# One matmul kernel, first token block computed with unsplit 32-bit operands, the weights' two parts made later

## The chip, the cores and the metric

The kernel runs on one core of one Trainium2 chip. The metric is the device time of one execution in microseconds (us), as the median of several executions. The engines are PE (matrix multiply), ACT (ScalarE), DVE (VectorE), POOL (GpSimd) and SP, which here only issues transfers.

## The reference

Three layers run one after the other on 4608 tokens of width 512:

```
q_s = softmax(q, axis=-1);  k_s = softmax(k, axis=tokens)      # 8 batches, 8 heads, 576 x 64
x   = q_s @ (k_s.T @ v)                                        # linear attention, heads joined to 512
h   = x @ w_in;  x = (h * cos(h)) @ w_out                      # 512 -> 2048 -> 512
do  = x @ w_skip > 0;  e = argmax(x[do] @ w_gate)              # 8 experts
out = x;  out[do] += gate * (relu(x @ w1[e]) @ w2[e])          # 512 -> 1024 -> 512
```

`w_in` and `w_out` come as 64-bit floats, all else as 32-bit floats.

## The kernel before

Tokens are taken in 12 blocks of 384. For each block the attention gives `xT`, the transposed input, and then 16 units follow, one for each 128 columns of the 2048. Unit `n` of the program is unit `c = n % 16` of block `j = n // 16`. In unit `n` PE runs `h_mm(n)` (12 matmuls of 384 columns, the h-tile), then `out_mm(n-3)` (9 matmuls of 512 columns into three accumulators `o`); `LAG = 3` is that distance. Between them lie `chain_a` and `chain_b` (h times cos h, on ACT and DVE) and `chain_c` (the product in two parts). The second expert stage (another matmul pair with its own loops) follows after the 12 blocks.

A product of 32-bit numbers is made from three matmuls in the faster type `float32r`: each operand is held as a high part (a cast on ACT) and a low part (a subtraction on DVE or POOL), and high-high, high-low and low-high are added. So x (`xh`, `xl`), the chain's product (`gh`, `gl`), the attention's kv matrix (`kvbh`, `kvbl`), q (`qh`, `ql`) and the weights (`W[m]`) all exist in two parts.

The 32 weight tiles `m` (even: a `w_in` slice for unit m/2, odd: a `w_out` slice) are loaded once, as 64-bit numbers, by `w_load`. `w_turn(m, done)` makes a 32-bit number from the bits (L148 on ACT, L149 and L154 on DVE, L155 on POOL) and, two steps later, splits the finished tile (L143 on ACT, L152 on DVE or, for tiles listed in `LOP`, on POOL). `w_step` does one such step; the tables `WA`, `WB`, `WC` say how many steps stand at which place of a unit of block 0, and `FP` where the next block's attention stands. The tile order is `order`: 0, 2, 4, then 1, 6, 3, 8 and so on. All engines run their instructions in the order in which the code writes them; there is no scheduler. The attention of block `j+1` is spread over the units of block `j` (`attention`, with the unit numbers in `A1` for block 1). In block 0 it also holds PE's, ACT's and DVE's time beside the weights.

Ahead of the first unit stands the attention of block 0 itself: `kmax_a` to `kmax_c`, `k_exp`, `kv_mm` for k and v, `q_max`, `q_exp`, `q_norm`, `q_trans`, `x_make` for q. `warm` issues matmuls on zeros.

Of the kernel before, what the change touches and what calls it, by code (L numbers as in the profile page):

```python
# [21 lines left out]
P = 128  # L22
# [20 lines left out]
A1 = (3, 3, 4, 6, 7, 9, 9, 9, 10, 8)  # L43
# [29 lines left out]
def body(ctx, tc, q, k, v, w_in, w_out, wg, w1, w2, cf, ct, ci, out):  # L73
# [51 lines left out]
    cw = {}  # L125
# [11 lines left out]
    def w_turn(m, done):  # L137


        if done is not None:  # L140
            f = cw.pop(done).bitcast(F32)
            t = W[done] = wp.tile([P, 2, DM], F32R, tag=f"w{done}", name="w")
            nc.scalar.copy(t[:, 0, :], f)  # L143
        if m is not None:
            w = cw[m].bitcast(U32).rearrange("p (n t) -> p n t", t=2)
            lw, hw = w[:, :, 0], w[:, :, 1]
            u = cw[m] = ws.tile([P, DM], U32, tag="u", name="u", bufs=4)
            nc.scalar.activation(lw, lw, AF.Copy, scale=2.0 ** -29)  # L148
            nc.vector.tensor_scalar(u, hw, 3, 0x3FFFFFF8, op0=ALU.logical_shift_left, op1=ALU.bitwise_and)  # L149
        if done is not None:  # L150
            eng = nc.gpsimd if done in LOP else nc.vector
            eng.tensor_tensor(t[:, 1, :], f, t.bitcast(F32)[:, 0, :], op=ALU.subtract)  # L152
        if m is not None:
            nc.vector.scalar_tensor_tensor(hw, hw, 0xC0000000, u, op0=ALU.bitwise_and, op1=ALU.bitwise_or)  # L154
            nc.gpsimd.tensor_tensor(u, hw, lw, op=ALU.add)  # L155
# [5 lines left out]
    at = [0]  # L161

    def w_step(n=1):
        for _ in range(n):
            t = at[0]
            at[0] += 1
            w_turn(order[t] if t < len(order) else None, order[t - 2] if 2 <= t < len(order) + 2 else None)
            if t + AHEAD < len(order):
                w_load(order[t + AHEAD])
# [54 lines left out]
    def kv_mm(b, i0=0, i1=NP):  # L224
        t, vv, n = kt, vt.rearrange("p c (h e) -> p c h e", h=H), i1 - i0
        ps = misc()[:, 0:n * (D + 1)].rearrange("p (i e) -> p i e", i=n)
        for i in range(n):
            for c in range(5):
                for u in range(2):
                    h = 2 * (i0 + i) + u  # L230
                    nc.tensor.matmul(ps[u * D:(u + 1) * D, i, :], t[:, c, h * D:(h + 1) * D], vv[:, c, h, :],
                                     start=c == 0, stop=c == 4)
        z = sp.tile([P, NP], F32, tag="kz", name="kz")[:, 0:n]
        nc.vector.tensor_scalar(z, ps[:, :, D], 1e-9, None, op0=ALU.add)
        nc.vector.reciprocal(z, z)
        t = sp.tile([P, DM], F32, tag="km", name="kv")[:, 0:n * D].rearrange("p (i e) -> p i e", i=n)
# [29 lines left out]
    def x_new(j):  # L266
        xT[j] = {s: p2.tile([P, KD, TB], F32R, tag="x" + s, name="x" + s) for s in "hl"}
# [24 lines left out]
    def q_trans(j, i):  # L292
        if j > 1:
            t = qt[j].rearrange("p g h d -> p (g h d)")[:, i * TB:(i + 1) * TB]
        else:
            t = (misc() if j else ps_h.tile([P, TB], F32, tag="h", name="h"))[:, 0:TB]
            for g in range(NG):
                nc.tensor.transpose(t[:, g * P:(g + 1) * P], qt[j][:, g, 2 * i:2 * i + 2, :].rearrange("p h d -> p (h d)"), ident)
        qT = st["qT", j, i] = {s: sp.tile([P, TB], F32R, tag="q" + s, name="q" + s, bufs=2) for s in "hl"}
        split(t, qT["h"], qT["l"])  # L300

    def x_make(j, i):
        qT = st.pop(("qT", j, i))
        ps = misc()
        c0 = 0
# [12 lines left out]
    def h_mm(n):  # L318
        j, c = divmod(n, NC)
        Hp[n] = ps_h.tile([P, TB], F32, tag="h", name="h")  # L320
        seq = [(a, b, kk) for kk in range(KD) for a, b in (("h", "h"), ("h", "l"), ("l", "h"))]
        for t, (a, b, kk) in enumerate(seq):
            nc.tensor.matmul(Hp[n], win(a, kk, c), xT[j][b][:, kk, :],  # L323
                             start=t == 0, stop=t == len(seq) - 1)
# [6 lines left out]
    def chain_b(n):  # L331
# [12 lines left out]
    def out_mm(n):  # L344
# [4 lines left out]
        for g in range(NG):  # L349
            for t, (a, b) in enumerate((("h", "h"), ("h", "l"), ("l", "h"))):  # L350
# [36 lines left out]
    def logits(j, rp):  # L387
# [5 lines left out]
        lt = R["lt", j] = rp.tile([P, TB], F32, tag="lt", name="lt", bufs=1)  # L393
# [112 lines left out]
    def init_table():  # L506
        z = ws.tile([P, E * CAP // P // 2, 2], I32, tag="z", name="z", bufs=1)
# [108 lines left out]
    def mlp(mp):  # L616
        XG = [mp.tile([P, G2, DM], F32, name=f"xg{i}") for i in range(2)]
# [254 lines left out]
    with tc.manual_schedule():  # L872
# [3 lines left out]
        for t in (kt, vt):  # L876
            nc.gpsimd.memset(t[64:P, 4, :], 0.0)
        for t in kvb:
            for s in "hl":
                nc.vector.memset(t[s].bitcast(F32), 0.0)  # L880
        load_k(0, 0, 2)
        load_q(0)
        load_k(0, 2, 4)
        load_v(0, 0, 2)
        for m in order[0:6]:
            w_load(m)
        load_v(0, 2, 4)
        for m in order[6:AHEAD]:
            w_load(m)
        nc.sync.dma_start(cfs, cf)  # L890
        nc.sync.dma_start(cis, ci)
        nc.sync.dma_start(tri, ct)
        nc.sync.dma_start(wgs, wg.rearrange("(k p) e -> p k e", p=P))
# [27 lines left out]
        x_make(0, 1)
        q_trans(0, 3)
        w_step()
        x_make(0, 2)
        x_make(0, 3)
        N = NB * NC
        for n in range(N + LAG):
# [32 lines left out]
            if j == 0:  # L960
                w_step(WB[c])
# [15 lines left out]
            if j == 0:  # L977
                w_step(WC[c])
# [94 lines left out]
```

## Time and profile before

| | |
|---|---|
| median of 3 executions | 1254.25 us (1253.8 to 1258.02) |
| the profiled execution | 1256.17 us, of which the span (first to last instruction) is 1254.3 us |
| PE, DVE, ACT, POOL busy | 96%, 60%, 57%, 33% of the span |
| TensorE's granted clock, mean | 0.986 of full speed |

The shares are means over the whole span. PE's 96% comes from a long stretch in which it never stops; the change lies in the first tenth of the span, where it does stop. The time of an execution is 1.9 us more than its span.

### The profile page before, as it was taken

Reading aid. Unit: us, or ns where it says so; the run is one execution under the profiler, and the core shown is the slowest. Engines: PE = TensorE matmul, PEld = TensorE weight load, DVE = VectorE, ACT = ScalarE, POOL = GpSimd, SP = SyncE. Lnnn points to the kernel's source line nnn. Section 1 sums busy time; section 2 is a strip of 40 time slices with the busy share of each in tenths; the row PEclk is TensorE's granted clock in tenths of the full one; section 3 lists DMA queues with packets and bytes.
Section 4 is the critical chain, followed back from the end, with each engine's and each line's share of the span. In section 5 each row is a group of like instructions: output and inputs, shape, how many; then the busy total and the mean of one; then the engine's idle time right before and its main releaser. Section 6 shows DMA issues by size and latency. Waiting matters only on the chain. (4 is left out here: it accounts for less than half of the span.)

```text
span 1254.3 us, 19798 instructions
## 1 busy us (share of the span) xinstructions
PE 1200.4 (96%) x7028; PEld 1056.8 (84%) x7028; DVE 752.6 (60%) x1506; ACT 719.3 (57%) x1393; POOL 411.5 (33%) x365
## 2 busy tenths in 40 slices
PE   7777999999999999999999999999999999999986
PEld 4666898888899898989988888898888889999984
DVE  7999735556354545635455564535565976676661
ACT  3667655655666665566655566665575555555541
POOL 3666542334324233432423334232120222122121
PEclk8889999999999999999999999999999999999998
DMA  9920222224212222321323232221054676677653
GB/s 306 366 82 1 58 39 69 51 65 110 48 56 51 73 57 64 109 34 61 59 36 97 65 97 35 73 51 26 26 168 144 184 244 226 220 227 235 214 153 146
DMA packets 209493, 138.75 MB, mean 111 GB/s; under 512 B 138200, under 2 KB 173272, under 8 KB 209376
## 3 DMA queue, kind: packets, MB, share of 16 engines
q1 hardware_dynamic: 204272, 125.13, 36.1%
q0 software_dynamic: 5104, 12.17, 2.8%
q8 instruction: 60, 0.98, 0.3%
q14 instruction: 57, 0.47, 0.1%
HBM read 106.35 MB, written 15.95 MB: 97 GB/s over the span
## 5 line engine op out<-in xcount | busy, mean ns | idle before, releaser
L323 PE MATMUL h<-xh,w 128*128 128x384 f32 x1536 | 435.9, 345 | 20.6 <-DVE w L152 6.6
L351 PE MATMUL o<-w,gh 128*128 128x512 f32 x1152 | 363.2, 396 | 2.6 <-ACT x L363 2.6
L323 PEld LDWEIGHTS h<-xh,w 128*128 128x128 f32 x1536 | 284.2, 190 | 38.3 <-DVE w L152 9.6
L342 POOL TENSOR_TENSOR gl<-a,gh 128x384 fp32r<-128x384 f32 x176 | 184.8, 1050 | 394.5 <-ACT gh L340 289.2
L323 PE MATMUL h<-xl,w 128*128 128x384 f32 x768 | 261.7, 341 | 0.1
L351 PEld LDWEIGHTS o<-w,gh 128*128 128x128 f32 x1152 | 214.8, 189 | 39.2 <-ACT x L363 3.9
L351 PE MATMUL o<-w,gl 128*128 128x512 f32 x576 | 229.0, 397 | 1.8 <-POOL gl L342 1.8
L335 DVE SCALAR_TENSOR_TENSOR a<-a,h 128x384 f32<-128x384 f32 x192 | 104.7, 545 | 191.9 <-ACT a L334 191.8
L328 ACT ACTIVATE a<-h 128x384 f32<-128x384 f32 x192 | 93.1, 485 | 182.5 <-PE h L323 106.2
L329 DVE SCALAR_TENSOR_TENSOR a<-a,h 128x384 f32<-128x384 f32 x192 | 105.4, 549 | 140.0 <-ACT a L328 139.9
L323 PEld LDWEIGHTS h<-xl,w 128*128 128x128 f32 x768 | 146.2, 190 | 5.6 <-DVE xl L314 0.6
L340 ACT CAST gh<-a 128x384 fp32r<-128x384 f32 x192 | 97.9, 510 | 72.4 <-DVE a L335 72.4
L844 PE MATMUL h<-xh,w 128*128 128x256 f32 x704 | 137.4, 280 | 0.3 <-DVE w L123 0.3
L351 PEld LDWEIGHTS o<-w,gl 128*128 128x128 f32 x576 | 108.5, 188 | 29.9 <-POOL gl L342 3.4
L123 DVE TENSOR_TENSOR w<-wr,w 128x512 fp32r<-128x512 f32 x192 | 123.9, 688 | 7.4 <-ACT w L122 1.9
L844 PEld LDWEIGHTS h<-xh,w 128*128 128x128 f32 x704 | 113.3, 189 | 4.1 <-ACT w L122 0.7
L855 PE MATMUL o<-w,gh 128*128 128x512 f32 x352 | 112.9, 401 | 0.0
L122 ACT CAST w<-wr 128x512 fp32r<-128x512 f32 x192 | 108.7, 618 | 1.8 <-DMA wr<-in_w 1.7
L333 ACT ACTIVATE a<-a 128x384 f32<-128x384 f32 x192 | 100.7, 524 | 11.0 <-DVE a L329 10.7
L334 ACT ACTIVATE a<-a 128x384 f32<-128x384 f32 x192 | 100.9, 525 | 6.1
L847 ACT ACTIVATE gh<-h 128x256 fp32r<-128x256 f32 x88 | 33.8, 384 | 120.4 <-PE h L844 96.9
L844 PE MATMUL h<-xl,w 128*128 128x256 f32 x352 | 98.7, 280 | 0.0
(220 smaller groups left out, 1460.1 us busy)
## 6 DMA issues: line engine op xcount, KB each, us to landing
wr<-in_w SPq DMA_DIRECT2D x101, 512.0 KB, 4.3
qt<-in_q SPq DMA_DIRECT2D x12, 768.0 KB, 5.7
out<-x SPq DMA_DIRECT2D x36, 256.0 KB, 2.2
wr<-in_w_in SPq DMA_DIRECT2D x16, 512.0 KB, 9.8
wr<-in_w_out SPq DMA_DIRECT2D x16, 512.0 KB, 11.2
xl<-x SPq DMA_DIRECT2D x160, 48.0 KB, 2.1
xh<-qt SPq DMA_DIRECT2D x160, 48.0 KB, 2.1
vt<-in_v SPq DMA_DIRECT2D x7, 1040.0 KB, 5.8
```

The costliest lines, as they stand in the source:

```text
L122: nc.scalar.copy(hi, src)
L123: nc.vector.tensor_tensor(lo, src, hi.bitcast(F32), op=ALU.subtract)
L323: nc.tensor.matmul(Hp[n], win(a, kk, c), xT[j][b][:, kk, :], start=t == 0, stop=t == len(seq) - 1)
L329: nc.vector.scalar_tensor_tensor(a, a, MAGIC, Hp[n], op0=ALU.subtract, op1=ALU.subtract)
L333: nc.scalar.activation(a, a, AF.Sin, scale=PI)
L334: nc.scalar.activation(a, a, AF.Square)
L335: nc.vector.scalar_tensor_tensor(a, a, 0.5, Hp.pop(n), op0=ALU.subtract, op1=ALU.mult)
L340: nc.scalar.copy(G[n]["h"], a)
L342: eng.tensor_tensor(G[n]["l"], a, G[n]["h"].bitcast(F32), op=ALU.subtract)
L351: nc.tensor.matmul(O[j][g], gg[a][:, g * P:(g + 1) * P], wout(b, c), start=c == 0 and t == 0, stop=c == NC - 1 and t == 2)
L844: nc.tensor.matmul(ps, win2(a, kk, c0, c * P, P), xt[b][:, kk, 0:T2], start=t == 0, stop=t == len(seq) - 1)
L855: nc.tensor.matmul(o[g], g_[a][:, g * P:(g + 1) * P], wout(b, c0 + c), start=c == 0 and t == 0, stop=c == NF - 1 and t == 2)
```

## The change

Block 0 does without the two parts. `x_new(0)`, `x_make(0, i)`, `q_trans(0, i)`, `h_mm`, `chain_b` and `out_mm` keep single 32-bit tiles (`xf`, `qf`, `kvf`, `gf`, and the turned weight `F[m]`) when `j == 0`, and one 32-bit matmul stands where three `float32r` matmuls stood. `w_turn` only turns; `F[m]` is written in place over the loaded tile. The split is a function of its own, `w_split`, called by `w_parts`: one tile in each unit from unit 4 to unit 15, then two and one in turn in block 1, always on ACT and DVE; a spare buffer (`SPARE`) lets a split tile go where the tile before it lay. `kv_parts` makes the two parts of kv for block 1 in unit 1.

Each unit of block 0 now has two `w_step`s at fixed places. Ahead of the units the order changes: both halves of k are loaded before q, the subtraction of q's maximum and half of `q_norm` run on DVE for block 0, ACT's table loads are called for early by a one-column instruction (`dum`), v's second half is loaded ahead of all but one weight, and `h_mm(0)` is issued in two halves. `init_table` (POOL) and four small loads move into unit 1, and its tile `z` now shares a buffer with `km`, the tile in which `kmax_a` takes its maxima. `lt` and one input tile of the last stage share other buffers.

```diff
+    def w_turn(m):
+        a = cw.pop(m)
...
+        u = ws.tile([P, DM], U32, tag="u", name="u", bufs=2)
+        nc.scalar.activation(lw, lw, AF.Copy, scale=2.0 ** -29)
+        nc.vector.tensor_scalar(u, hw, 3, 0x3FFFFFF8, op0=ALU.logical_shift_left, op1=ALU.bitwise_and)
+        nc.vector.scalar_tensor_tensor(hw, hw, 0xC0000000, u, op0=ALU.bitwise_and, op1=ALU.bitwise_or)
+        nc.gpsimd.tensor_tensor(a.bitcast(U32)[:, 0:DM], hw, lw, op=ALU.add)
+        F[m] = a.bitcast(F32)[:, 0:DM]
+
+    def w_split(m):
+        f = F.pop(m)
+        t = W[m] = wp.tile([P, 2, DM], F32R, tag="w" + room_w.pop(0), name="w")
+        nc.scalar.copy(t[:, 0, :], f)
+        nc.vector.tensor_tensor(t[:, 1, :], f, t.bitcast(F32)[:, 0, :], op=ALU.subtract)
+        room_w.append(str(m))
...
+    def kv_parts():
+        for u in range(2):
+            r = slice(u * D, (u + 1) * D)
+            hi, lo = (kvb[0][s][r, :, r] for s in "hl")
+            split(kvf[r, :, r], hi, lo)
...
     def x_make(j, i):
+        if j == 0:
+            nc.tensor.matmul(ps[:, 0:TB], kvf[:, i, :], qT["f"], start=True, stop=True)
+            nc.scalar.activation(xT[j]["f"][:, i, :], ps[:, 0:TB], AF.Copy, scale=INV2PI)
+            return
...
+        for kk in range(k0, k1):
+            if j == 0:
+                nc.tensor.matmul(Hp[n], F[2 * c][:, kk * P:(kk + 1) * P], xT[j]["f"][:, kk, :],
+                                 start=kk == 0, stop=kk == KD - 1)
+                continue
...
+        g = a
+        if n < NC:
+            g = p3.tile([P, TB], F32, tag="gh", name="gf")
+            G[n] = {"f": g}
+        nc.vector.scalar_tensor_tensor(g, a, 0.5, Hp.pop(n), op0=ALU.subtract, op1=ALU.mult)
...
+            if j == 0:
+                nc.tensor.matmul(O[j][g], gg["f"][:, g * P:(g + 1) * P], F[2 * c + 1], start=c == 0, stop=c == NC - 1)
+                continue
...
+        z = sp.tile([P, DM], F32, tag="km", name="z").bitcast(I32)[:, 0:2 * n].rearrange("p (c t) -> p c t", t=2)
...
+        q_max(0, 0)
+        kmax_b(0, 2, 4)
+        q_max(0, 1)
+        q_exp(0)
+        warm(4)
+        kmax_c(0, 2, 4)
+        k_exp(0, 2, 4)
+        nc.scalar.activation(dum, dum, AF.Sin)
+        warm(4)
+        kv_mm(0, 0, 2)
+        q_norm(0)
+        warm(4)
+        kv_mm(0, 2, 4)
+        w_step()
+        warm(4)
+        q_trans(0, 0)
+        x_new(0)
+        q_trans(0, 1)
...
+        x_make(0, 2)
+        h_mm(0, 0, 2)
         w_step()
-        x_make(0, 2)
         x_make(0, 3)
+        h_mm(0, 2, 4)
...
-                w_step(WB[c])
+                w_step()
...
-                w_step(WC[c])
+            if n >= SPL and at[1] < 2 * NC:
+                w_parts(1 if n < NC or c % 2 else 2)
+            if n == 1:
+                init_table()
+                kv_parts()
```

What the change does to the instructions shows in the order on three engines. On PE, where the attention ends and the first units begin, the program before has the last group of x (three matmuls of the two parts of kv and q), then the h-tile of unit 0 from parts of x and of the weight:

```order
L310 MATMUL m<-qh,kvbh_91 128x384
L310 MATMUL m<-ql,kvbh_91 128x384
L310 MATMUL m<-qh,kvbl_92 128x384
L323 MATMUL h<-xh,w 128x384
L323 MATMUL h<-xl,w 128x384
L323 MATMUL h<-xh,w 128x384 x2
```

In the changed program the same place reads as follows; `wr` is the loaded tile, in which the turned weight now lies:

```order
L320 MATMUL h<-ident,qt 128x128 x3
L332 MATMUL m<-qf,kvf 128x384
L357 MATMUL h<-xf,wr 128x384 x2
L332 MATMUL m<-qf,kvf 128x384
L357 MATMUL h<-xf,wr 128x384 x14
L395 MATMUL o_452<-wr,gf 128x512
```

One matmul stands for three, the first half of unit 0's h-tile moved ahead of the last group of x, and nothing but turned weights is waited for there.

On DVE, unit 4 of block 0 before (the chain's two instructions, then turns L149 and L154 around a split L152):

```order
L335 SCALAR_TENSOR_TENSOR a<-a,h 128x384
L329 SCALAR_TENSOR_TENSOR a<-a,h 128x384
L149 TENSOR_SCALAR u<-wr 128x512
L154 SCALAR_TENSOR_TENSOR wr<-wr,u 128x512
L149 TENSOR_SCALAR u<-wr 128x512
L152 TENSOR_TENSOR w<-u,w 128x512
L154 SCALAR_TENSOR_TENSOR wr<-wr,u 128x512
```

and the same unit in the changed program (L202 is one step of the next block's `kmax_a`):

```order
L377 SCALAR_TENSOR_TENSOR gf<-a,h 128x384
L367 SCALAR_TENSOR_TENSOR a<-a,h 128x384
L142 TENSOR_SCALAR u<-wr 128x512
L143 SCALAR_TENSOR_TENSOR wr<-wr,u 128x512
L142 TENSOR_SCALAR u<-wr 128x512
L143 SCALAR_TENSOR_TENSOR wr<-wr,u 128x512
L202 TENSOR_TENSOR km<-km,kt 128x512
L152 TENSOR_TENSOR w<-wr,w 128x512
```

The split moved to the unit's end, where the tile that it makes is first read in block 1.

On POOL, in units 3 to 6 of block 0 before, the turn's addition (L155), the product's low part (L342) and the splits listed in `LOP` (L152) take turns:

```order
L155 TENSOR_TENSOR u<-wr 128x512 x2
L342 TENSOR_TENSOR gl<-a,gh 128x384
L152 TENSOR_TENSOR w<-u,w 128x512
L155 TENSOR_TENSOR u<-wr 128x512 x2
L342 TENSOR_TENSOR gl<-a,gh 128x384
L152 TENSOR_TENSOR w<-u,w 128x512
```

and in the changed program, from the last turn ahead of unit 2 on (L557, L558 and L561 are `init_table`, L265 is block 1's `q_max`):

```order
L144 TENSOR_TENSOR wr<-wr 128x512 x7
L557 MEMSET z 128x152
L558 MEMSET z 128x152
L561 DMA tab<-z 128x304 x2
L144 TENSOR_TENSOR wr<-wr 128x512 x10
L265 TENSOR_TENSOR qt<-qt,qm 128x1536
L144 TENSOR_TENSOR wr<-wr 128x512 x6
```

Low parts and splits left POOL for the whole of block 0, and the table's transfer moved from ahead of the units to behind the seventh turn.

## Rows read from the trace of the kernel before

**Rows 1.** Busy time of each engine by stage, with granted clock and DMA.
```profile
core 0: us, PE busy (x) PEld busy (x) DVE busy (x) ACT busy (x) POOL busy (x), PEclk, DMA share, GB/s
0.00:32.42 32.42, 23.54 (x150) 14.07 (x151) 24.58 (x46) 13.02 (x23) 11.12 (x17) 0.84 0.97 308
32.42:45.92 13.50, 8.96 (x37) 7.49 (x37) 12.17 (x18) 7.14 (x15) 6.70 (x6) 0.87 1.05 353
45.92:138.85 92.93, 72.37 (x402) 61.37 (x402) 89.67 (x117) 62.63 (x120) 66.03 (x51) 0.93 0.31 105
138.85:206.00 67.15, 67.15 (x345) 59.91 (x344) 31.52 (x70) 40.75 (x78) 24.38 (x22) 1.00 0.20 36
```

**Rows 2.** PE's timeline: start and length in us; units 0, 3, 16, 17 begin.
```profile
32.42 0.34 PE L323 MATMUL h<-xh,w 128*128 128x384 f32 x1
...
45.92 0.44 PE L323 MATMUL h<-xh,w 128*128 128x384 f32 x1 [2.51 <-DVE a L335]
...
138.85 0.34 PE L323 MATMUL h<-xh,w 128*128 128x384 f32 x1
...
140.97 0.63 PE L351 MATMUL o<-w,gh 128*128 128x512 f32 x2
...
143.06 0.34 PE L323 MATMUL h<-xh,w 128*128 128x384 f32 x1
```

**Rows 3.** PE's waits from 32.4 to 139 us: total, times, longest.
```profile
PE h L323 <- DVE w L152: 6.6, 7, 2.2
PE h L323 <- DVE a L335: 5.9, 3, 2.5
PE h L323 <- POOL w L152: 5.1, 2, 4.1
```

**Rows 4.** 32-bit matmuls: ns min/median/max of a record, then runs of PE's timeline.
```profile
L392 PE MATMUL m<-x,wgs x80: 486/498/510, 189.3 to 858.0; 128*32 128x384 f32 x80
...
L214 PEld LDWEIGHTS m<-ident,kmx x64: 187/190/337, 7.6 to 754.0; 128*128 128x128 f32 x64
L214 PE MATMUL m<-ident,kmx x64: 271/275/582, 7.6 to 754.1; 128*128 128x128 f32 x64
...
88.83 1.05 PE L214 MATMUL m<-ident,kmx 128*128 128x128 f32 x8
...
101.98 2.55 PE L231 MATMUL m<-vt,kt 128*64 128x65 f32 x80
```

**Rows 5.** Groups by line, 32.4 to 140 us: busy us, mean ns, idle before.
```profile
L154 DVE SCALAR_TENSOR_TENSOR wr<-wr,u 128x512 uint32<-128x512 uint32 x30 | 34.7, 1157 | 0.3
L152 DVE TENSOR_TENSOR w<-u,w 128x512 fp32r<-128x512 f32 x20 | 23.5, 1174 | 1.1 <-ACT w L143 0.9
L149 DVE TENSOR_SCALAR u<-wr 128x512 uint32<-128x512 uint32 x29 | 15.7, 542 | 0.0
...
L155 POOL TENSOR_TENSOR u<-wr 128x512 uint32<-128x512 uint32 x30 | 36.2, 1206 | 29.1 <-issue 7.8 <-DVE wr L154 5.2 <-ACT xh L313 4.7
L152 POOL TENSOR_TENSOR w<-u,w 128x512 fp32r<-128x512 f32 x10 | 16.7, 1675 | 2.1 <-DVE a L329 1.6 <-ACT w L143 0.5
L342 POOL TENSOR_TENSOR gl<-a,gh 128x384 fp32r<-128x384 f32 x14 | 16.4, 1169 | 2.4 <-ACT gh L340 2.4
```

**Rows 6.** DVE and POOL timelines near 49 us.
```profile
48.82 0.41 DVE L149 TENSOR_SCALAR u<-wr 128x512 uint32<-128x512 uint32 x1
49.15 0.68 DVE L152 TENSOR_TENSOR w<-u,w 128x512 fp32r<-128x512 f32 x1
49.75 1.53 DVE L154 SCALAR_TENSOR_TENSOR wr<-wr,u 128x512 uint32<-128x512 uint32 x1
...
49.12 1.60 POOL L155 TENSOR_TENSOR u<-wr 128x512 uint32<-128x512 uint32 x1 [1.38 <-ACT a L333]
```

**Rows 7.** DVE and ACT timelines ahead of the first unit.
```profile
10.66 2.73 DVE L200 TENSOR_TENSOR km<-kt 128x256 f32<-128x256 f32 x1 [0.46 <-DMA kt<-in_k]
...
17.03 1.74 DVE L255 TENSOR_REDUCE qs<-qt 128x24 f32<-128x1536 f32 x1
...
26.87 0.49 ACT L313 ACTIVATE xh<-m 128x384 fp32r<-128x384 f32 x1
27.38 1.28 ACT L918 ACT_TABLE_LOAD   x1
```

**Rows 8.** DMA issues up to 150 us: KB each, median us to landing.
```profile
tab<-z POOLq DMA_DIRECT2D x2, 152.0 KB, 5.6
```

**Rows 9.** PE's waits from 139 to 275 us.
```profile
PE o L351 <- POOL gl L342: 0.8, 1, 0.8
PE o L351 <- ACT x L363: 0.6, 1, 0.6
```

More of the change, by code (lines that the diff above doesn't have):

```diff
@@ L123, in split @@
         nc.vector.tensor_tensor(lo, src, hi.bitcast(F32), op=ALU.subtract)
-    cw = {}
+    cw, F = {}, {}
+    room_w = [f"x{i}" for i in range(SPARE)]
     def w_load(m):
@@ L135, in w_load @@
             nc.sync.dma_start(a, w_out[c * P:(c + 1) * P, :])
[L137 to L155, printed above, removed]
+    def w_turn(m):
+        a = cw.pop(m)
+        w = a.bitcast(U32).rearrange("p (n t) -> p n t", t=2)
+        lw, hw = w[:, :, 0], w[:, :, 1]
+        u = ws.tile([P, DM], U32, tag="u", name="u", bufs=2)
[10 more added lines that the diff above has]
+        room_w.append(str(m))
     order = [0, 2, 4]
@@ L160, in body, with w_parts @@
     order = [m for m in order if m < 2 * NC]
-    at = [0]
+    at = [0, 0]
     def w_step(n=1):
[L164 to L169, printed above, removed]
+        for m in order[at[0]:at[0] + n]:
+            w_turn(m)
+        for m in order[at[0] + AHEAD:at[0] + n + AHEAD]:
+            w_load(m)
+        at[0] += n
+    def w_parts(n=1):
+        for m in order[at[1]:at[1] + n]:
+            w_split(m)
+        at[1] += n
     qt = {}
@@ L316, in body, with h_mm @@
     A, G, Hp, O = {}, {}, {}, {}
-    def h_mm(n):
+    three = (("h", "h"), ("h", "l"), ("l", "h"))
+    def h_mm(n, k0=0, k1=KD):
         j, c = divmod(n, NC)
[L320 to L324, printed above, removed]
+        if k0 == 0:
+            Hp[n] = ps_h.tile([P, TB], F32, tag="h", name="h")
+        for kk in range(k0, k1):
+            if j == 0:
+                nc.tensor.matmul(Hp[n], F[2 * c][:, kk * P:(kk + 1) * P], xT[j]["f"][:, kk, :],
+                                 start=kk == 0, stop=kk == KD - 1)
+                continue
+            for t, (a, b) in enumerate(three):
+                nc.tensor.matmul(Hp[n], win(a, kk, c), xT[j][b][:, kk, :],
+                                 start=kk == 0 and t == 0, stop=kk == KD - 1 and t == 2)
     def chain_a(n):
@@ L349, in out_mm @@
         for g in range(NG):
[L350 removed]
+            if j == 0:
+                nc.tensor.matmul(O[j][g], gg["f"][:, g * P:(g + 1) * P], F[2 * c + 1], start=c == 0, stop=c == NC - 1)
+                continue
+            for t, (a, b) in enumerate(three):
                 nc.tensor.matmul(O[j][g], gg[a][:, g * P:(g + 1) * P], wout(b, c),
@@ L616, in mlp @@
     def mlp(mp):
-        XG = [mp.tile([P, G2, DM], F32, name=f"xg{i}") for i in range(2)]
+        XG = [mp.tile([P, G2, DM], F32, name="xg0"), wp.tile([P, G2, DM], F32, tag="w" + room_w[0], name="xg1")]
         ID, IC = ([mp.tile([P, G2, 2], I32, name=f"{t}{i}") for i in range(2)] for t in ("id", "ic"))
@@ L877, in body @@
             nc.gpsimd.memset(t[64:P, 4, :], 0.0)
+        dum = const.tile([P, 1], F32, name="dum")
+        nc.vector.memset(dum, 0.0)
+        nc.vector.memset(kvf, 0.0)
         for t in kvb:
@@ L880, in body @@
                 nc.vector.memset(t[s].bitcast(F32), 0.0)
+        nc.scalar.activation(dum, dum, AF.Exp)
         load_k(0, 0, 2)
+        load_k(0, 2, 4)
         load_q(0)
-        load_k(0, 2, 4)
         load_v(0, 0, 2)
-        for m in order[0:6]:
+        w_load(order[0])
+        load_v(0, 2, 4)
+        for m in order[1:AHEAD]:
             w_load(m)
[L887 to L893, printed above, removed]
         kmax_a(0, 0, 2)
```

79 lines of the change are left out of this document (40 added, 39 removed).

## The prediction

> **What bounds the kernel now.** I read the stages first. From the start of unit 16 PE is busy without a gap at the full clock, 67.15 of 67.15 us, and DVE is busy for half of that; ahead of it, in units 3 to 15, PE has 72.37 us of work in 92.93 us at a mean clock of 0.93, while DVE is busy for 89.67 [rows 1]. So nearly everything after unit 16 is PE's own work, and the change can gain only in the first 139 us. Read the unit starts next: unit 0 begins at 32.42, unit 3 at 45.92, unit 16 at 138.85, and a unit in undisturbed running takes 143.06 - 138.85 = 4.21 us, of which the h-tile is 2.12 and the out matmuls 2.09 [rows 2]. Thirteen such units would be 54.7 us, not 92.93. The waits say what is missing: PE's longest in block 0 are for the split of a weight (L152, on DVE or POOL) and for the chain's product on DVE [rows 3]. Ahead of the units the transfers are saturated (share 0.97 and 1.05, 308 and 353 GB/s), but in units 3 to 15 their share is 0.31 [rows 1]: weights arrive well before they are turned, so DVE with POOL beside it sets block 0's pace.
>
> Why these two are slow is seen in two durations. L154 takes 0.68 us when nothing is beside it, as L152 does at 49.15, but 1.157 on average [rows 5, 6]. At 49.75 it takes 1.53: it ends 0.56 us after POOL's L155 ends at 50.72, and that one took 1.60 because it had waited for L152 [rows 6]. The two engines hold each other up, so a POOL instruction is also a DVE cost.
>
> **What the matmuls cost now.** No full 32-bit matmul of 384 or 512 columns stands in the trace. The nearest are L392 (384 columns, 498 ns) and L214 (128 columns, 275 ns) [rows 4]: 223 ns for 256 columns is 0.87 ns a column. L214 comes from four calls and has eight records, so one call makes two records, and eight records in 1.05 us are (1.05 - 0.275) / 7 = 0.111 us apart, again 0.87 ns a column, with their 190 ns weight loads hidden [rows 4]. So I cost a 32-bit matmul at 2 x 0.87 ns a column: 0.67 us for 384 and 0.89 us for 512. A unit is 4 x 0.67 + 3 x 0.89 = 5.35 us, against 4.21: the new unit has a third of the matmuls and takes 1.14 us longer on PE. From below: two streams at two clocks a column of 2.4 GHz and no overhead give 5.12. From above: if the load were not hidden, 14 x 0.19 = 2.7 more, 8.0.
>
> The Trainium skill ("FP8 and Floating Point Precision", TensorE Precision Notes) says that a true 32-bit product is four passes through the array; against three split passes this speaks against the change on PE. Taken as four thirds of 4.21 it gives an estimate of 5.6 us a unit, 13 x 0.25 = 3.3 us over my sum; the rows above stand nearer to 5.35.
>
> **Units 3 to 15.** PE's work two ways. From before: 72.37 + 13 x 1.14 = 87.2, less what the low clock added, 0.07 x 92.93 = 6.5 [rows 1], is 80.7. From parts: 13 x 5.35 = 69.6, plus the next block's attention, 48 short matmul records, counted in the order of block 0, at 0.111 (5.3) and `kv_mm` 2.55 [rows 4], is 77.4; it leaves out the tails at PE's stops. I take 79.
>
> Is DVE fast enough? It loses the splits that were on the way: 8 of 20 leave block 0, 8 x 1.17 = 9.4 us, and 25 turns in this stretch become 23, 2 x 1.70 = 3.4 [rows 5]. That alone is 89.67 - 12.8 = 76.9, with POOL in the way as before. But POOL loses its splits (16.7 us) and low parts (16.4) of some 66 us [rows 1, 5], about half, so half of the blocking goes: a turn's blocked 1.70 (0.542 + 1.157) falls toward 0.33 + 0.60 by the starts in [rows 6], and 23 turns alone give back 23 x 0.77 / 2 = 9. DVE comes to 68, under PE's 79. ACT does two turns and one split a unit less the old product cast, and was busy for 62.63 [rows 1]; it stays behind too. A tile is turned about two units before its h-tile and nearly three before its out matmuls, 10 us of slack. Two places eat it: the first `kmax_a` in unit 2 writes `km`, which `z`'s transfer still reads (5.6 us to landing [rows 8]), with all of unit 3's turns behind it on DVE, and units 6 to 9, where block 1's maxima, sums and exponentials are queued ahead of the turns. I take 2 us of PE waits for both; nothing from below, and from above half of the present idle, 20.6 / 2 = 10.3 [rows 1]. Stage: 79 + 2 = 81 instead of 92.9, a gain of 11.9.
>
> **Ahead of the units.** Before, DVE's first maximum of k's second half took 2.73 us behind POOL's subtraction of q's maximum, q's sums start at 17.03, and unit 0 starts 15.4 us later [rows 2, 7]. Now that subtraction is DVE's own (1536 columns, as long as the sum's 1.74), and q is loaded third, so I put q's sums 1.3 us later, at 18.3. But from there to unit 0 remain: sum 1.74, small steps 0.5, half of the normalization 0.9, transposes 0.5, then for two groups of x, overlapped, a copy of about 0.5, a matmul of 0.67, a copy of 0.49, a second and third matmul: 7.2 us to 25.5. What goes is a split behind each copy, two of three matmuls a group, kv's split, and the sine table's 1.28 us load in the middle of the copies [rows 7], which now runs under `kv_mm`. The first turn must be there too: DVE reaches it about 22, POOL ends it by 25. Unit 0's h-tile then needs 2.67 and waits about 1.3 for the fourth group; units 1 and 2 have no out matmuls, 2.67 each, so unit 3 starts at 25.5 + 9.3, about 35, instead of 45.92: 10.9. If PE stays at the low clock here (0.84 before [rows 1]) it is 4 us worse; if the transfers let q in earlier, 2 better. The other loads moved to unit 1 go behind ten weights, and nothing needs them before block 1.
>
> **What is given back.** Units 16 to 18 still issue block 0's last out matmuls: 9 x (0.89 - 2.09 / 3) = 1.7. Block 1 takes over 20 splits, 1.5 a unit: a 0.69 us subtraction on DVE (31.52 of 67.15 busy) and a cast about as long on ACT (40.75) [rows 1]. PE stops there for only 0.8 and 0.6 us now [rows 9]; I take 1 us more, zero from below.
>
> Sum: 10.9 + 11.9 - 1.7 - 1.0 = 20.1 less. The profiled execution, 1256.17, goes to 1236; its span to 1234. The runs' median is 1.9 below the profiled one, so from 1254.25 I forecast **1234**.
>
> **The rivals.**
> *PE still waits for the turns* in block 0's second half: 10.3 us of idle stay, not 2, so 1242. For it speaks that DVE is in 97% use now and that the attention is moved one unit later for some steps; against it, that its load falls by a quarter. Chance 0.2.
>
> *32-bit matmuls are cheaper than rows suggest*, one record being all that costs: a unit is 2.7 us, DVE's 68 plus its present idle of 3 sets the stage, 71 instead of 81, and the given-back 1.7 turns into a gain of 2: 1220. Against it speaks the 0.111 us spacing of two records a call. Chance 0.04. The Trainium skill ("Perfetto Trace Analysis", Engine Utilization) halves TensorE's output rate for one 32-bit mode, which, if it were all, would be this case.
>
> *Loads of full 32-bit weights stand in the open.* Before, each load lay under a matmul; if 128 x 128 loads of this type do not, 14 x 0.19 = 2.7 us a unit is added in 16 units and half that in some early ones, about 40: 1274, slower. It decides from 1.4 us a unit on, half of a load in the open. Against it: L214's eight records with 128-column loads are 0.111 apart though each load takes 0.19 [rows 4]. Chance 0.05.
>
> *Block 1 pays it all back.* If each of the 20 splits stops PE for its cast and subtraction, 20 x 1.3 = 26 us instead of 1: 1259, no change. It would show as PE waiting for L152 in block 1. Against it: 10 us of slack and engines half idle. Chance 0.05.
>
> **How the numbers follow.** The forecast has chance 0.66, its own range 1228 to 1240 (ramp 4 worse or 2 better, 77.4 or 80.7 on PE, waits 0 to 5). The first rival and the low end of the second widen it: 1223 to 1247 leaves out the last two, half of the second and some tails, about 0.17. This kernel's runs tell about 0.5%, 6.3 us, from no change. Below 1248 lie the forecast and two rivals, 0.90, of which I keep 0.88; same 0.06, slower 0.06.
>
> **What would show it.** In the changed profile: 32-bit h records about 0.33 us apart and out records 0.45, two a call; unit 3 starting near 35 and unit 16 near 116; PE near 98% busy between at clock 1.0; L143 near 0.8 us on average; no wait over 2 us for L144 or L377. I would be wrong if records are over 0.4 and 0.55 apart, if PE waits over 10 us in block 0, or if PE waits for L152 in block 1.

## The result

The changed kernel takes 1240.35 us in the median (1239.13 to 1241.79, 4 runs) against 1254.86 for the kernel before on the same chip: a ratio of 0.9881, 95% interval 0.9859 to 0.9903. That is 14.5 us less, where 20.1 were forecast. Its profiled execution took 1239.63 us with a span of 1237.8, 16.5 less than before; the rest of this text counts in spans.

The stages first, cut where the same units begin (columns as in [rows 1]): the ramp, units 0 to 2, units 3 to 15, then unit 16 to the reading out of block 1.

```profile
core 0: us, PE busy (x) PEld busy (x) DVE busy (x) ACT busy (x) POOL busy (x), PEclk, DMA share, GB/s
0.00:23.90 23.90, 17.70 (x144) 9.80 (x145) 20.82 (x40) 10.72 (x17) 4.88 (x10) 1.00 0.94 308
23.90:32.78 8.88, 8.86 (x28) 4.77 (x26) 6.67 (x11) 6.81 (x15) 4.28 (x4) 1.00 1.06 356
32.78:118.96 86.18, 79.12 (x311) 43.30 (x311) 79.53 (x120) 52.01 (x96) 38.34 (x34) 0.96 0.47 161
118.96:210.30 91.34, 88.81 (x429) 74.57 (x427) 55.92 (x104) 57.07 (x112) 27.97 (x23) 1.00 0.21 48
```

Unit 3 starts at 32.78 instead of 45.92, unit 16 at 118.96 instead of 138.85 [rows 2], so units 3 to 15 take 86.2 us instead of 92.9 [rows 1]. The stage from unit 16 to the end of block 1 took 86.75 before (138.85 to 225.60) and now takes 91.34: there 4.6 us are given back. PE is busy 92% of units 3 to 15, not 98%, at a clock of 0.96, and DVE is busy for 79.53 us, more than PE. The waits of PE behind that, from 25 to 130 us (in total, times, longest):

```profile
PE m L320 <- DVE kv L244: 2.9, 1, 2.9
PE h L357 <- issue: 2.2, 1, 2.2
PE m L208 <- DVE km L202: 1.8, 1, 1.8
```

Before, PE waited 25.0 us in 17 stops from 32.4 to 139 us: the 17.6 us of [rows 3], 2.9 for the cast of a weight, 0.6 for ql, and these two, which have nothing to do with a weight:

```profile
PE m L298 <- DVE kv L237: 2.0, 1, 2.0
PE m L206 <- DVE km L200: 1.9, 1, 1.9
```

So the stops for weights and for the chain's product went, all but one; the two for the attention's kv and km were there before and stayed, one of them longer. All three that are left come from DVE: two name it; the one called "issue" ends at 45.43, 0.09 us behind DVE's L377 (44.79 and 0.55 long), which frees the PSUM buffer of the h-tile and stands behind DVE's own wait for the table (below). At 2.18 us it is over the 2 us that the prediction allowed a wait for L377. PE's timeline shows what a stop costs beside its length: the h-tiles at 45.43 and 93.90 follow one, the other four lines are undisturbed.

```profile
35.36 2.74 PE L395 MATMUL o<-wr,gf 128*128 128x512 f32 x6
37.94 2.74 PE L357 MATMUL h<-xf,wr 128*128 128x384 f32 x8
...
45.43 4.51 PE L357 MATMUL h<-xf,wr 128*128 128x384 f32 x8 [2.18 <-issue]
...
59.99 2.75 PE L357 MATMUL h<-xf,wr 128*128 128x384 f32 x8
62.57 2.74 PE L395 MATMUL o<-wr,gf 128*128 128x512 f32 x6
...
93.90 4.28 PE L357 MATMUL h<-xf,wr 128*128 128x384 f32 x8
```

From start to start, eight h records take 62.57 - 59.99 = 2.58 us and six out records 37.94 - 35.36 = 2.58: 0.322 and 0.430 us a record, two records a matmul, and a unit is 5.16 us. The h-tile at 45.43 took 4.35 instead, that at 93.90 took 4.12: 3.3 us more for both, and the granted clock of the two stretches around them (43.26 to 49.78 and 90.30 to 98.02) is 0.74 and 0.78 of full speed, that is, the lower of its two levels, 1.2 instead of 2.4 GHz, for part of each.

DVE and POOL, 25 to 130 us, by line (columns as in [rows 5], whose L154, L149 and L155 are now L143, L142 and L144):

```profile
L144 POOL TENSOR_TENSOR wr<-wr 128x512 uint32<-128x512 uint32 x31 | 34.5, 1112 | 46.6 <-DVE wr L143 20.9 <-ACT a L372 12.1 <-ACT qh L119 4.3
L143 DVE SCALAR_TENSOR_TENSOR wr<-wr,u 128x512 uint32<-128x512 uint32 x30 | 32.7, 1091 | 1.0
L142 DVE TENSOR_SCALAR u<-wr 128x512 uint32<-128x512 uint32 x29 | 14.3, 492 | 0.0
L152 DVE TENSOR_TENSOR w<-wr,w 128x512 fp32r<-128x512 f32 x15 | 12.8, 856 | 1.2 <-ACT w L151 1.2
```

L143 fell only from 1157 to 1091 ns, though POOL's busy time in units 3 to 15 fell by 42%, from 66.03 to 38.34 us; the split, L152, fell from 1174 to 856. Two pieces of DVE's and POOL's timelines show why, and how it reaches PE. The first is near 39 us.

```profile
38.35 0.69 DVE L143 SCALAR_TENSOR_TENSOR wr<-wr,u 128x512 uint32<-128x512 uint32 x1
38.96 0.42 DVE L142 TENSOR_SCALAR u<-wr 128x512 uint32<-128x512 uint32 x1
39.42 1.41 DVE L143 SCALAR_TENSOR_TENSOR wr<-wr,u 128x512 uint32<-128x512 uint32 x1
...
39.19 1.09 POOL L144 TENSOR_TENSOR wr<-wr 128x512 uint32<-128x512 uint32 x1 [0.50 <-ACT a L372]
...
44.18 0.69 DVE L202 TENSOR_TENSOR km<-kt 128x512 f32<-128x512 f32 x1 [3.35 <-DMA tab<-z]
```

The first turn's addition on POOL (39.19 to 40.28) lies over the second turn's L143, which takes 1.41 us instead of 0.69 and ends 0.55 after the addition. The Trainium skill ("SBUF — State Buffer", Who interferes with whom) states that a DVE instruction with two SBUF inputs contends with a GpSimd instruction that reads SBUF, and calls the port pair that they share an exclusive lock. By that rule a unit whose two turns follow each other has at least one held-up instruction however idle POOL is otherwise; the trace agrees, 1.41 beside 0.69. The last line is the wait that the prediction named: km's first step waits 3.35 us for the table's transfer.

The second piece is DVE ahead of PE's longest stop, which ends at 93.39.

```profile
88.08 0.77 DVE L142 TENSOR_SCALAR u<-wr 128x512 uint32<-128x512 uint32 x1
88.88 1.84 DVE L143 SCALAR_TENSOR_TENSOR wr<-wr,u 128x512 uint32<-128x512 uint32 x1
90.65 0.41 DVE L142 TENSOR_SCALAR u<-wr 128x512 uint32<-128x512 uint32 x1
91.10 1.41 DVE L143 SCALAR_TENSOR_TENSOR wr<-wr,u 128x512 uint32<-128x512 uint32 x1
92.43 0.15 DVE L236 TENSOR_SCALAR kz<-m 128x4 f32<-128x4 f32 x1
92.61 0.18 DVE L237 RECIPROCAL kz<-kz 128x4 f32<-128x4 f32 x1
92.83 0.42 DVE L244 TENSOR_TENSOR kv<-m,kz 128x256 f32<-128x256 f32 x1
```

The two turns, 4.35 us with both L143 held up (the first beside the attention's own normalization of q on POOL, L280, the second beside an addition), stand in DVE's queue ahead of the three short instructions that PE waits for. PE does not stop for a weight; it stops for the attention, which is queued behind the weights.

### The profile page after: what moved, and what is told of

It reads as the page before. It is cut to its first block, busy times and chain, and to the rows that moved or that the text cites. A ratio compares the mean times of both kernels' runs of the same rounds, so it can differ in the third digit from the quotient of the medians.

```text
span 1237.8 us, 19513 instructions
## 1 busy us (share of the span) xinstructions
PE 1204.2 (97%) x6912; PEld 1031.3 (83%) x6912; DVE 747.2 (60%) x1513; ACT 713.1 (58%) x1376; POOL 370.5 (30%) x336
## 5 line engine op out<-in xcount | busy, mean ns | idle before, releaser
L361 PE MATMUL h<-xh,w 128*128 128x384 f32 x1408 | 395.7, 342 | 0.0
L398 PE MATMUL o<-w,gh 128*128 128x512 f32 x1056 | 331.8, 395 | 2.6 <-ACT x L410 2.6
L386 POOL TENSOR_TENSOR gl<-a,gh 128x384 fp32r<-128x384 f32 x160 | 167.0, 1044 | 405.5 <-ACT gh L384 300.1
L361 PEld LDWEIGHTS h<-xh,w 128*128 128x128 f32 x1408 | 257.9, 188 | 12.8 <-issue 6.7
L361 PE MATMUL h<-xl,w 128*128 128x384 f32 x704 | 237.8, 338 | 0.1
L398 PEld LDWEIGHTS o<-w,gh 128*128 128x128 f32 x1056 | 196.0, 188 | 36.1 <-ACT x L410 3.9
L398 PE MATMUL o<-w,gl 128*128 128x512 f32 x528 | 209.4, 397 | 1.6 <-POOL gl L386 1.6
L377 DVE SCALAR_TENSOR_TENSOR a<-a,h 128x384 f32<-128x384 f32 x176 | 96.0, 545 | 178.5 <-ACT a L372 178.4
L367 DVE SCALAR_TENSOR_TENSOR a<-a,h 128x384 f32<-128x384 f32 x192 | 105.2, 548 | 133.4 <-ACT a L366 133.2
L361 PEld LDWEIGHTS h<-xl,w 128*128 128x128 f32 x704 | 132.4, 188 | 5.8 <-issue 1.0
L120 DVE TENSOR_TENSOR w<-wr,w 128x512 fp32r<-128x512 f32 x192 | 123.7, 687 | 7.4 <-ACT w L119 1.7
L398 PEld LDWEIGHTS o<-w,gl 128*128 128x128 f32 x528 | 99.2, 188 | 27.6 <-POOL gl L386 3.4
L893 PEld LDWEIGHTS h<-xh,w 128*128 128x128 f32 x704 | 113.4, 189 | 4.3 <-ACT w L119 0.9
L904 PE MATMUL o<-w,gh 128*128 128x512 f32 x352 | 112.9, 401 | 0.0
L119 ACT CAST w<-wr 128x512 fp32r<-128x512 f32 x192 | 108.7, 619 | 1.4 <-DMA wr<-in_w 1.4
```

Of the source, the lines that this page charges most:

```text
L119: nc.scalar.copy(hi, src)
L120: nc.vector.tensor_tensor(lo, src, hi.bitcast(F32), op=ALU.subtract)
L361: nc.tensor.matmul(Hp[n], win(a, kk, c), xT[j][b][:, kk, :], start=kk == 0 and t == 0, stop=kk == KD - 1 and t == 2)
L367: nc.vector.scalar_tensor_tensor(a, a, MAGIC, Hp[n], op0=ALU.subtract, op1=ALU.subtract)
L377: nc.vector.scalar_tensor_tensor(g, a, 0.5, Hp.pop(n), op0=ALU.subtract, op1=ALU.mult)
L386: eng.tensor_tensor(G[n]["l"], a, G[n]["h"].bitcast(F32), op=ALU.subtract)
```

## The experiments

Theory 1, formed on this trace: DVE is full, because each addition on POOL holds up DVE's next instruction, and PE meets the full queue wherever the attention needs DVE. Theory 2: a few single events or places in DVE's queue (the table's transfer, the order) make the stops, and its load would fit. "Unit 16" is its start; block 1 is measured from there to its reading out, 91.3 us in the changed kernel. These marks come from one profiled execution of each run, and they vary: unit 0 starts at 23.5 to 25.3 us in runs whose code ahead of it is the same, and stretches of PE at the low clock come and go (last section). Where it matters, the way from unit 0's start to unit 16's is given, 95.1 us in the changed kernel; differences under some 2 us are not read.

**The table later.** The one wait with a name is taken away.

```diff
-            if n == 1:
+            if n == 7:
                 init_table()
```

> init_table stands in unit 7 instead of unit 1, so z's transfer no longer stands ahead of the first km. Theory of single events (PE's lost time in block 0 comes from two queue events on DVE, z's transfer and block 1's kv): the 3.35 us wait of km goes, and with it PE's 2.18 us wait before unit 5, the 1.77 us that unit 5 loses at the low clock and the 1.82 us before unit 7: 5.8 us, unit 16 starts near 113.2, time near 1235. Theory of a full DVE (DVE is the bound from 44 to 93 us because POOL blocks it): only DVE's idle 3.35 us comes back, unit 16 near 115.6, time near 1237. If neither, no change.

1236.19 us, ratio 0.984 (0.9822 to 0.9857); unit 16 at 114.53, 4.4 earlier. The 3.35 us wait and the low clock are gone; PE still stops:

```profile
PE m L208 <- DVE km L202: 2.5, 1, 2.5
PE m L320 <- DVE kv L244: 2.3, 1, 2.3
PE m L340 <- DVE ql L120: 1.1, 1, 1.1
```

So the table's transfer was worth 4 us, and it was not the whole: three stops stay with nothing late but DVE. Of the 4.4 us, 3.35 are PE's work at the low clock (PE is busy for 75.77 us of units 3 to 15 instead of 79.12). Both marks lie between what the two theories had asked for, so this run does not choose.

**One q step later.** Block 1's second group of q is moved from unit 11 to unit 12.

```diff
-Q1 = (11, 11, 12, 13)
+Q1 = (11, 12, 12, 13)
```

> Block 1's second q_trans moves from unit 11 to unit 12, so PE no longer waits there for DVE to read kv from PSUM. Single events: the 2.94 us wait and the 1.54 us at the low clock behind it go, 4.4 us, unit 16 near 114.5, time near 1236. Full DVE: DVE is as late as before, PE meets it at the next h-tile or x group; at most the low clock's 1.5 us comes back, time 1239 to 1240.

1247.78 us, 0.9929 (0.9913 to 0.9946), unit 16 at 126.88: slower than the changed kernel, which neither theory had foreseen. The stops moved and grew:

```profile
PE m L320 <- DVE xl L344: 4.2, 1, 4.2
PE h L357 <- issue: 3.3, 1, 3.3
PE m L340 <- DVE ql L120: 2.2, 1, 2.2
PE m L340 <- ACT qh L119: 2.0, 1, 2.0
PE m L208 <- DVE km L202: 1.8, 1, 1.8
```

The waits for L344, L120 and L119 are for PSUM buffers or parts that DVE and ACT read late. The run tells that a place in the queue matters by several us, but it does not tell the theories apart.

**The addition on DVE.** POOL does not turn at all.

```diff
-        nc.gpsimd.tensor_tensor(a.bitcast(U32)[:, 0:DM], hw, lw, op=ALU.add)
+        nc.vector.tensor_tensor(a.bitcast(U32)[:, 0:DM], hw, lw, op=ALU.bitwise_or)
```

> The turn's addition on POOL (L144) becomes a bitwise or on DVE, so nothing on POOL blocks DVE in a turn; an or drops a carry, so a few weights differ in their last bits. DVE gets about 30 x 0.60 = 18 us of work and loses the blocking, which I work out as 17 us (L143 1.091 - 0.68, 30 times; L152 0.856 - 0.68, 15 times; L142 0.492 - 0.42, 29 times). Full DVE with blocking as its cost: no change within 2 us, L143 at 0.69 on average. If blocking costs nothing on the path: 8 us slower or more. If it costs more than it shows: faster.

1245.05 us, 0.9916 (0.9896 to 0.9936), unit 16 at 123.11, 4.2 later; PE waits 5.2 us for km and 5.1 for kv.

```profile
L143 DVE SCALAR_TENSOR_TENSOR wr<-wr,u 128x512 uint32<-128x512 uint32 x30 | 22.0, 732 | 1.0
L144 DVE TENSOR_TENSOR wr<-wr 128x512 uint32<-128x512 uint32 x31 | 21.5, 693 | 3.3
L142 DVE TENSOR_SCALAR u<-wr 128x512 uint32<-128x512 uint32 x30 | 14.6, 485 | 0.0
L152 DVE TENSOR_TENSOR w<-wr,w 128x512 fp32r<-128x512 f32 x14 | 9.5, 680 | 0.9 <-ACT w L151 0.9
```

Without POOL, L143 takes 732 ns and L152 680, so its additions cost DVE 32.7 - 22.0 = 10.7 us on L143 and 15 x 0.176 = 2.6 on L152. Doing them itself costs 21.5. DVE has 8 us more, and 4 of them come out at PE. That is neither of the expected outcomes (within 2 us, or 8 and more): taking the hold-up away with POOL's work did not pay for doing the work on DVE.

**Splits later.** Six splits go from block 0 to block 1.

```diff
-SPL = 4
+SPL = 10
...
-                w_parts(1 if n < NC or c % 2 else 2)
+                w_parts(1 if n < NC else 2)
```

> Splits begin in unit 10 instead of 4, and block 1 does two a unit: 6 splits leave units 4 to 9. Full DVE: 6 x 0.86 = 5.1 us less DVE work in the stretch where it never rests, unit 16 about 4 us earlier (115), less about 1 us of new waits in block 1, time near 1237. Single events: the splits are not what PE waits for, unit 16 stays near 119, time 1240 to 1241.

1244.97 us, 0.9913 (0.9895 to 0.9931). Unit 16 is at 114.26, 4.7 earlier, about what six splits at 0.856 us are (5.1); in units 3 to 15 DVE's busy time falls by 4.5 us (79.53 to 74.99) and the stage by as much (86.18 to 81.65). Block 1 takes 100.0 us instead of 91.3, where 1 us had been expected, and the time is longer, with these stops of PE:

```profile
PE m L340 <- ACT qh L119: 2.9, 1, 2.9
PE h L361 <- DVE a L377: 2.5, 1, 2.5
PE m L470 <- DVE oh L463: 1.5, 1, 1.5
PE m L448 <- ACT lt L442: 0.9, 1, 0.9
```

A split in block 0 cost 0.8 us, moved to block 1 it cost 1.45 (8.7 / 6). The clock has a part in both: it stayed at 1.00 in units 3 to 15, where 3.6 us of PE's busy time went, and was 0.95 in block 1, where 3.5 came on top. In block 1 this happened though DVE is busy there for 61 of the 100 us: by the names of the waits, which no run tested further, short instructions of DVE and ACT, queued behind two splits on end, come late.

**Turns apart.** In block 0 a unit's first turn is issued ahead of the chain, so that two turns no longer follow each other.

```diff
                 h_mm(n)
+            if j == 0:
+                w_step()
             if 0 <= n - 1 < N:
                 chain_b(n - 1)
...
                 chain_c(n - 1)
-            if j == 0:
-                w_step()
```

> In block 0 the unit's first turn moves ahead of the chain, so that on DVE two instructions on PSUM (L377, L367) stand between two turns, and POOL's addition of the first turn runs beside them instead of blocking L143 of the second. Full DVE: L143 falls from 1.09 us on average to about 0.75, DVE gets 14 x 0.7 = 10 us back in the stretch where it never rests, unit 16 starts near 113 instead of 119, time near 1235. If the blocking is not on the path: no change within 1.5 us.

1238.35 us, 0.9855 (0.9838 to 0.9871), unit 16 at 117.37. Unit 0 started at 25.32 in this execution, and from there it is 92.1 us to unit 16, 3.0 less than in the changed kernel. L143 falls to 825 ns, but L142 rises from 492 to 703: most of the held-up time passes to the next instruction, 1.53 us a turn instead of 1.58. The expected 10 us did not come.

**Both.** Turns apart and the table later.

> Turns apart as above and init_table in unit 7. Full DVE: both add, until PE's own work is the bound (unit 3 at 32.8 + 13 x 5.16 + 7.6 of attention = 107.5): unit 16 near 110, time near 1232. If both only remove the same PE waits, not more than the better of the two alone, about 1235.

1234.64 us, 0.9832 (0.9815 to 0.9848), unit 16 at 114.17, 89.0 behind unit 0 (the table alone: 90.7). It has the lowest median of the versions that leave nothing out, but its interval overlaps that of the table alone, so that both gains add is not shown.

**The old ramp.** The table later, and ahead of unit 0 the old order: q's subtraction and normalization on POOL, the loads, table loads and the first unit's calls where they were.

> The changed kernel with the old order up to the first unit (loads, q's subtraction and normalization on POOL, table loads where they fall), init_table in unit 7: to be set beside the run with init_table late alone, 1236.2. If the block carries its start through: unit 0 near 29.5 instead of 25.8, unit 16 as much later, about 118, time near 1240. If a full DVE or the weights' arrival sets unit 16 whatever the start: unit 16 near 115, time 1236 to 1237.

1243.47 us, 0.9892 (0.9876 to 0.9909). Unit 0 starts at 30.4 instead of 23.9 and unit 16 at 121.09, 6.6 later than with the table alone; from unit 0 to unit 16 it is 90.7 us in both. (The 25.8 in the expectation is where the second half of unit 0's tile began.) What the ramp gains stays to the end, and the new order is about 6.6 us of it, known to some 2 us; the rest of the ramp's 13 is left for the single 32-bit products, which were not tried by themselves.

**Splits spread.** As "both", with block 1's splits in three of four units singly.

```diff
-                w_parts(1 if n < NC or c % 2 else 2)
+                w_parts(1 if n < NC or c % 4 else 2)
```

> As turns apart with init_table late, and block 1's 20 splits spread, two only in every fourth unit, until unit 31. If splits in block 1 are what its new PE waits come from (26 splits at two a unit cost it 8.7 us, 20 at one and a half some 1.7): 1 to 2 us better than the run without, time near 1231. If block 1's waits come from attention and routing alone: no change.

1235.92 us, 0.983 (0.9814 to 0.9847), the same as "both"; block 1 takes 92.7 us instead of 91.2. The way in which the splits are dealt out does not decide block 1's loss.

**The attention first.** As "both", and a unit's second turn is issued behind the attention.

```diff
-            if j == 0:
-                w_step()
...
             run(f.pop(c, []))
+            if j == 0:
+                w_step()
```

> As the last but one kernel (the unit's two turns apart, the table later), and in block 0 a unit's second turn is issued behind the next block's attention instead of ahead of it. DVE's work is the same; only what waits behind what changes. Theory 1 (DVE is full, by POOL's additions): the waits for the attention's km and kv (0.8 and 2.5 us) shrink by up to a turn, 1.5 us each, but full work meets PE elsewhere; unit 16 from 114.2 to between 112.5 and 114.2, time 1633 to 1635 less 400, that is 1233 to 1235. Theory 2 (DVE's load would fit, PE's stops come from the order of its queue alone): both waits go, with the stretch at low clock behind them, unit 16 comes to 109 to 110, time 1229 to 1230.

1238.36 us, 0.9867 (0.9852 to 0.9882), unit 16 at 115.11, 91.4 behind unit 0 instead of 89.0. The wait for km is gone, that for kv stays (2.7), and a new one of 1.9 appears ahead of an h-tile. A turn went from 1.55 to 1.71 us (L142 at 772 ns, L143 at 936). Neither number came: theory 1 had asked for 1233 to 1235, theory 2 for 1229 to 1230. The order alone does not free PE.

**Splits from unit 2.** As "the attention first", with `SPL = 2`.

> As the kernel with the attention ahead of the second turn, and the splits begin in unit 2 instead of 4: two splits move from block 1 into units 2 and 3, where DVE was busy for 7.85 of 10.48 us. If each split in block 1 costs what moving six there cost (8.7 us, 1.45 each) and DVE has room in units 2 and 3, unit 16 starts within 1 us of the same time and block 1 is 1.5 to 3 us shorter: time 1 to 3 us less. If DVE is full from unit 2 on, unit 16 is 1.7 later and the time within 1 us of the same.

1236.3 us, 0.9847 (0.9833 to 0.986); the intervals overlap, and the two spans (1233.9 and 1234.8) stand the other way round. From unit 0's start to unit 16 it is 0.8 longer, block 1 is 1.0 shorter. No difference is shown.

**No addition.** The table later, and POOL's addition is left out of every turn, so each weight lacks its low 3 bits.

```diff
-        nc.vector.scalar_tensor_tensor(hw, hw, 0xC0000000, u, op0=ALU.bitwise_and, op1=ALU.bitwise_or)
-        nc.gpsimd.tensor_tensor(a.bitcast(U32)[:, 0:DM], hw, lw, op=ALU.add)
+        nc.vector.scalar_tensor_tensor(a.bitcast(U32)[:, 0:DM], hw, 0xC0000000, u, op0=ALU.bitwise_and, op1=ALU.bitwise_or)
```

> The kernel with the table later, with POOL's addition left out of every turn: the low 3 bits of each weight's number are missing, DVE's instruction writes the weight where the addition did. DVE has as many instructions as before. Theory 1 (POOL's additions hold DVE up by 0.4 to 0.5 us each, and that makes DVE full): L143 falls from 1.07 to about 0.70, L152 from 0.87 to 0.68, 14 us of DVE's work in all go, PE's waits of 5.9 us go but for under 1, and unit 16 comes from 114.5 to 107.5 to 109 (107.5 is PE's own work behind unit 3's start); time 1229 to 1231. Theory 2 (the stops come from the order of DVE's queue, not from its load): a stop shrinks by a turn's 0.4 to 0.8 only, unit 16 at 112 to 113.

1229.16 us, 0.9798 (0.9782 to 0.9814). Units 3 to 15 and then block 1:

```profile
32.09:107.91 75.82, 75.05 (x312) 41.84 (x310) 67.31 (x119) 52.02 (x96) 8.03 (x7) 1.00 0.54 187
107.91:199.93 92.02, 88.81 (x429) 74.58 (x427) 55.93 (x104) 57.06 (x111) 27.93 (x23) 1.00 0.21 48
```

With the same instructions on DVE, PE is busy for 75.05 of 75.82 us; the stage with the addition and the table later took 81.80 (32.73 to 114.53). DVE's busy time is 67.31 instead of 78.81, and PE's waits are 0.5 and 0.3 us. The clock is 1.00 in both stages. This is theory 1's number (unit 16 at 107.5 to 109, time 1229 to 1231), and it settles it: POOL's additions, by what they do to DVE, cost units 3 to 15 some 6 us. L143 writes to another place in this run, which does nothing by itself: it takes 729 ns, against 732 with the addition on DVE, where it wrote in place. A missing addition also makes each turn shorter by itself; but no stop was for a turned weight, so that cannot be the gain.

## Why the prediction held, and where it failed

The time lies in the range, on the side forecast. The forecast's own range ended at 1240, just below 1240.35; it is the range widened for the rivals that holds it. By its terms, against the spans:

| term | forecast | measured |
|---|---|---|
| ahead of unit 3 | -10.9 | -13.1 |
| units 3 to 15 | -11.9 | -6.7 |
| units 16 to 18 | +1.7 | +1.4 |
| the rest of block 1 | +1.0 | +3.2 |
| behind block 1 | 0 | -1.2 |
| sum | -20.1 | -16.5 |

The medians differ by 2 us less than the profiled executions, since the one of before was 1.3 above its median and the one after is 0.7 below.

**The matmul's cost** was right in its mechanism, two records a matmul with the weight loads hidden; its size is the lower bound given, 5.12, almost exactly: 5.16, not 5.35. The Trainium skill ("FP8 and Floating Point Precision", TensorE Precision Notes) has four passes for a true 32-bit product, and the trace agrees: 0.322 us for 384 columns is two clocks a column of 2.4 GHz, and two records make four. The estimate of 5.6 drawn from it was too high because it scaled a unit of before, 4.21 us, which is more than three such passes (3 x 1.28 = 3.84). The two rivals on matmul prices are refuted by these records.

**The ramp** came out 2.2 better: unit 0 at 23.90 instead of 25.5. DVE's q sums start at 16.73, not 18.3, and PE's clock is 1.00 all through the ramp, where it had been 0.84; the old order (the run above) accounts for about half of the 13 us.

**The step that failed** is "DVE comes to 68, under PE's 79", with 2 us of waits: DVE measured 79.53. It failed in what was counted off. These are the turns and splits on DVE in units 3 to 15, before and then after:

```profile
L154 DVE SCALAR_TENSOR_TENSOR wr<-wr,u 128x512 uint32<-128x512 uint32 x25 | 29.5, 1179 | 0.3
L152 DVE TENSOR_TENSOR w<-u,w 128x512 fp32r<-128x512 f32 x16 | 19.1, 1191 | 1.1 <-ACT w L143 0.9
L149 DVE TENSOR_SCALAR u<-wr 128x512 uint32<-128x512 uint32 x25 | 14.1, 562 | 0.0
...
L143 DVE SCALAR_TENSOR_TENSOR wr<-wr,u 128x512 uint32<-128x512 uint32 x27 | 29.2, 1082 | 0.9
L142 DVE TENSOR_SCALAR u<-wr 128x512 uint32<-128x512 uint32 x27 | 13.4, 497 | 0.0
L152 DVE TENSOR_TENSOR w<-wr,w 128x512 fp32r<-128x512 f32 x12 | 10.4, 866 | 0.2 <-ACT w L151 0.2
```

The forecast let 25 turns become 23, the number that the program writes behind the start of unit 3. But DVE runs behind PE: it had done five of the 32 when PE began unit 3, so 27 fell into the stage. And it took eight of 20 splits off, counted from 32.4 to 140 us, from a busy time of 89.67 us that holds only 16; four left. Four turns at 1.74 us and four splits at 1.19 are 11.7 us, which is the miss of 11.5; a new split of kv (1.6 us) and a relief somewhat larger than forecast about cancel.

"Half of the blocking goes" was right in its sum, though not where it was put. Reckoned as what L154, L149, L152 and km's steps (their lines after the change likewise) took beyond their undisturbed 0.69, 0.42, 0.68 and 0.68 us, DVE was held up for some 27 us in this stage before and 15 after, a fall of 45% beside POOL's 42%. The turns gave little, 1.74 to 1.58 us each and L143 still at 1.09 against the 0.8 forecast, because every addition stayed; splits (1.19 to 0.87 each) and km's four steps (5.7 to 2.8 us together) gave the rest. That DVE at 68 would have been enough is shown: left without the additions it stood at 67.31, and PE waited 0.8 us. Whether the four turns fewer would have done the same was not tried.

PE's own work in the stage is 75 us, not 79, so the stage of 86.2 holds 11 us of loss and not 2: 6.9 of waits, 3.3 of low clock behind two of them, the rest in small pieces. That is the first rival's size (10.3) with a different object: PE waits for the attention that is queued behind the turns, not for turned weights. That PE's work was over-costed by 4 us hid nearly half of this error; that was luck.

Within this stage, the wait for `z`'s transfer was named, but taken at 2 us together with the maxima; without it unit 16 started 4.4 us earlier, the low clock included.

**Block 1's loss** was under-costed, 3.2 us instead of 1. Idle time of PE from unit 16 to the reading out rose from 0.9 to 2.5 us, 1.2 of it for L484, whose instruction stands behind two splits on DVE; no wait is for L152 itself. The other 1.5 us are PE's busy time, and which instructions they belong to was not found: neither dealing the splits out singly nor moving two of them away changed it measurably.

## What to carry to other kernels

When you count work off an engine's busy time, count the instructions in the very stretch that the busy time was read from, by their starts in the trace and not by their place in the program: an engine that runs behind carries its backlog into the next stage. Cost what two engines hold each other up by from the instructions that stay. Before taking work off a critical engine's matmuls, ask which short instructions stand behind long ones on the feeding engine; those become the next stops. Leaving a suspect out wholly, with the other engine's instructions kept, told in one run what the runs of reordering did not.

## What the runs showed of the hardware beside that

In block 0 the granted clock fell after PE had waited 2.18 and 2.94 us (h-tiles of 4.35 and 4.12 us instead of 2.58), and not after a wait of 1.82 (59.49, then 2.58). The length of a wait alone does not decide it: with the table later PE waited 2.5 and 2.3 us and the clock of units 3 to 15 was 1.00. "Both" and "splits spread" run the same code up to unit 16 and had nearly the same waits in it (1.3, 2.5, 0.8 and 1.2, 2.5, 0.8 us), with a clock of 1.00 and of 0.98.

An instruction of DVE with one SBUF input is held up by POOL as well. In the kernel with the turns apart, L142 took 2.99 us beside POOL's long subtraction; alone it takes 0.41:

```profile
66.28 2.99 DVE L142 TENSOR_SCALAR u<-wr 128x512 uint32<-128x512 uint32 x1
69.31 0.69 DVE L143 SCALAR_TENSOR_TENSOR wr<-wr,u 128x512 uint32<-128x512 uint32 x1
...
65.90 3.09 POOL L265 TENSOR_TENSOR qt<-qt,qm 128x1536 f32<-128x1536 f32 x1 [1.22 <-DVE qm L262]
```

It ends at 69.27, 0.28 behind POOL's end at 68.99. Another L142, at 70.84, took 0.61 us beside an addition (70.13, 1.04 long) and ended 0.28 behind that too. This fits what setting the turns apart did: it passed most of the hold-up on.
